# Mixing the first block straight from PSUM with 257-column products instead of differences, and ending VectorE's sums of k squares one group sooner

## Chip, cores, metric

One core of one Trainium2 chip. The metric is the device time of one execution in microseconds (us). All runs named here were fast runs; the granted TensorE clock of the profiled ones was 0.998 to 1.0. Times are medians, with lowest and highest and the number of runs. The profiled execution is one of the runs (for the kernel before a further one, 505.44). PE is TensorE, the matmul engine. Tiles whose names end in `_ps` (and `bank`) lie in PSUM, the other tiles in SBUF; to evacuate a tile is to copy it from PSUM to SBUF. A load is said to land at the time of PE's first instruction on its data, 0.03 to 0.05 us behind the landing itself, unless the text says that PE came later.

## The reference

Two parts, one behind the other. Sizes: 4 batches, 6208 rows, C = 256, hidden width 1024.

```python
def _attn_ref(q, k, v, tau):
    qn = q / (np.linalg.norm(q, axis=1, keepdims=True) + 1e-06)
    kn = k / (np.linalg.norm(k, axis=1, keepdims=True) + 1e-06)
    s = kn.transpose(0, 2, 1) @ qn / tau          # 256 x 256 per batch
    s = s - s.max(-1, keepdims=True)
    a = np.exp(s)
    a /= a.sum(-1, keepdims=True) + 1e-09
    return v @ a

def _moe_ref(x, mu_k, mu_r, w_k, w_v, w_r):       # x is what _attn_ref returns
    x_prev = ...                                  # x shifted down by one row, zero first
    xk = mu_k * x + (1.0 - mu_k) * x_prev
    xr = mu_r * x + (1.0 - mu_r) * x_prev
    k = np.maximum(xk @ w_k, 0.0)
    v = k * k @ w_v
    r = 1.0 / (1.0 + np.exp(-(xr @ w_r)))
    return r * v
```

Batch 0's q and k must be read whole before any x exists. That is the head of the program. The kernel then goes through blocks of 512 rows: x, the mixtures xk and xr, the two matmuls with the square between them, the gate.

## The kernel before: the parts that matter

Block 0 is mixed in a way of its own. PE computes x in PSUM, and the difference of neighbouring rows by multiplying a difference of v. ScalarE copies x to SBUF, and VectorE makes `xk = (mu - 1) * difference + x` (H is 256, half a block):

```python
def difference(a):                                     # VectorE, twice
    c = slice(a * H, (a + 1) * H)
    nc.vector.tensor_tensor(dv[:, :, c], vT0[:, :, a * H + 1:(a + 1) * H + 1], vT0[:, :, c], op=OP.subtract)

def product(a, ih):
    ...
    for dh in range(2):
        for t, src in zip(pairs[a], (vT0[:, ih, a * H + 1:(a + 1) * H + 1], dv[:, ih, a * H:(a + 1) * H])):
            nc.tensor.matmul(t[:, dh], a_sb[:, 0, ih, dh * P:(dh + 1) * P], src, ...)
    if ih:
        for dh in (0, 1):
            nc.scalar.copy(xT[:, dh, a * H + 1:(a + 1) * H + 1], pairs[a][0][:, dh])

def mix_first(key, a, dh):                             # one VectorE instruction
    c = slice(a * H, (a + 1) * H)
    m = less[:, dh:dh + 1] if key == "xk" else less[:, 2 + dh:3 + dh]
    nc.vector.scalar_tensor_tensor(st[0, key][:, dh, c], st[0, "ps"][a][1][:, dh], m,
                                   st[0, "x"][:, dh, a * H + 1:(a + 1) * H + 1], op0=OP.mult, op1=OP.add)
```

The schedule around the first blocks (i = -1 is the step that still belongs to the head; block 1 is `i + 2`):

```python
if j > 0 and 0 <= i + 1 < NBLK:
    square(i + 1, j - 1)               # VectorE: kk = kr * kr, four 512-column pieces in one go
...
if 0 < i + 2 < NBLK:
    n = i + 2
    if j in (0, 2) and full:
        x_half(n, int(j > 0))          # PE, then ScalarE evacuates xT
    if j == 3:
        mix_delta(n)                   # VectorE: delta = x - x_prev, needs both halves of xT
    if j in (4, 5):
        mix(n, "xk", int(j > 4))       # VectorE
if j in (0, 2) and i == -1:
    for a in range(2):
        mix_first("xr", a, int(j > 0)) # VectorE
```

Two things also matter: `kr` has two tiles, so ScalarE may write block 1's first `kr` only when the square of block 0's first four pieces has read the old one; and `group_cast` of group `NB - 1` contains `v_mark()`, a VectorE memset that releases the loads of v and of the weights on GpSimdE's queue.

## Time and profile before

| | value | how to read it |
|---|---|---|
| time | 505.31 us (505.25 to 505.42, 3 runs) | 2% is 10.1 us |
| profiled span | 503.67 us | |
| PE busy | 481.4 us, 96% of the span | no room except in the head |
| VectorE, ScalarE busy | 429.0 and 428.8 us, 85% each | averages; in the head each of them is at times what the others wait for |
| first 50 us | PE waits for casts, norms, softmax, mixing | the only place where this change acts |

The prediction shows the lines that carry this: the table of stretches, the chain of waits up to 49.17 us, and VectorE's timeline.

### The profile page before, as it was taken

To read this page: it belongs to the slowest core of one execution; us is meant where nothing else is said; L and a number is where in the kernel's file an instruction comes from. 1 tells how busy PE (TensorE), PEld (TensorE's weight loads), DVE (VectorE), ACT (ScalarE), POOL (GpSimd) and SP (SyncE) were. 2 spreads that over 40 slices of the span, in tenths; PEclk is the share of its full clock that TensorE was granted. 3 is DMA by queue.
4 is the path that set the end of the run, shared out by engine and by line. 5 is a ranking of instruction groups with operands and counts; after the bars stand their busy time and mean duration, and the time that the engine had idled before them with its cause. 6 is when DMAs were issued, how large, how long until landed. Compare 5 with 4: busy or idle time off the path is not lost.

```text
span 503.7 us, 9289 instructions
## 1 busy us (share of the span) xinstructions
PE 481.4 (96%) x3429; PEld 330.8 (66%) x3429; DVE 429.0 (85%) x789; ACT 428.8 (85%) x872; POOL 97.3 (19%) x143
## 2 busy tenths in 40 slices
PE   1689999999999999999999999999999999999996
PEld 1355677667666666776676676666666666666675
DVE  2778899998988998899889899899888787878784
ACT  4788999899989989888999898988888878788784
POOL 0044332222233222122123322110031010000000
PEclk9999999999999999999999999999999999999999
DMA  8999999999999999996699999982295858343123
GB/s 324 419 311 192 183 143 188 142 183 199 210 216 196 217 177 179 146 208 110 142 195 146 181 184 185 163 145 73 64 208 97 160 88 151 80 103 89 55 72 105
DMA packets 131558, 83.46 MB, mean 166 GB/s; under 512 B 50548, under 2 KB 125624, under 8 KB 130488
## 3 DMA queue, kind: packets, MB, share of 16 engines
q0 software_dynamic: 55840, 33.01, 51.7%
q1 hardware_dynamic: 75352, 49.59, 42.9%
q8 instruction: 27, 0.44, 0.4%
q10 hardware_dynamic: 320, 0.26, 0.2%
q14 instruction: 19, 0.16, 0.1%
HBM read 78.71 MB, written 25.43 MB: 207 GB/s over the span
## 4 chain that ended last, share of the span: by engine, by line
PE 87%; DMA 6%; ACT 3%; DVE 2%; issue 1%; SPq 1%; ACTq 0%; DVEq 0%
PE vr_ps L603 32%; PE kT_ps L571 32%; PE vr_ps L599 8%; PE xT_ps L465 8%; PE s_ps L293 6%; DMA vT<-v_bf 3%; DMA f<-in_k_dram 3%; ACT k L160 1%; ACT qk L155 1%; SPq L125 1%; PE s_ps L199 0%; PE y_ps L643 0%; DVE xk L556 0%; PE st_ps L353 0%; DVE k L167 0%
## 5 line engine op out<-in xcount | busy, mean ns | idle before, releaser
L576 ACT ACTIVATE kr<-kT_ps 128x512 bf16<-128x512 f32 (+1 forms) x390 | 234.5, 604 | 32.9 <-PE kT_ps L571 29.0
L603 PE MATMUL vr_ps<-w_v_sb,kk 128*128 128x256 bf16 x1536 | 230.2, 273 | 0.0
L571 PE MATMUL kT_ps<-xk,w_k_sb 128*128 128x512 bf16 (+1 forms) x780 | 230.0, 377 | 0.2 <-DVE xk L556 0.2
L603 PEld LDWEIGHTS <-kk 128*128 128x128 bf16 x1536 | 150.3, 98 | 57.3
L584 DVE TENSOR_TENSOR kk<-kr 128x2048 bf16<-128x2048 bf16 (+1 forms) x148 | 125.8, 851 | 0.2 <-ACT kr L576 0.2
L613 DVE SCALAR_TENSOR_TENSOR res<-res,vr_ps 128x256 f32<-128x256 f32 x192 | 80.0, 417 | 50.9 <-ACT res L612 50.9
L571 PEld LDWEIGHTS <-w_k_sb 128*128 128x128 bf16 x780 | 75.5, 98 | 27.5 <-issue 0.6
L612 ACT ACTIVATE res<-vr_ps 128x256 f32<-128x256 f32 x192 | 76.5, 399 | 2.3 <-PE vr_ps L603 1.3
L599 PE MATMUL vr_ps<-w_r_sb,xr 128*128 128x256 bf16 x384 | 73.3, 273 | 0.0
L467 ACT CAST xT<-xT_ps 128x512 bf16<-128x512 f32 x94 | 55.9, 594 | 20.0 <-PE xT_ps L465 19.7
L556 DVE SCALAR_TENSOR_TENSOR xr<-delta,mu_t,xT 128x512 bf16<-128x512 bf16 x94 | 70.0, 746 | 0.0
L556 DVE SCALAR_TENSOR_TENSOR xk<-delta,mu_t,xT 128x512 bf16<-128x512 bf16 x94 | 70.0, 746 | 0.0
L599 PEld LDWEIGHTS <-xr 128*128 128x128 bf16 x384 | 37.6, 98 | 44.7 <-issue 0.4
L133 POOL DMA_DIRECT2D qk<-in_q_dram x39 | 26.1, 668 | 159.8 <-ACT kr L576 129.8
L465 PE MATMUL xT_ps<-vT,a_sb 128*128 128x512 bf16 x188 | 55.9, 379 | 0.2 <-DMA vT<-v_bf 0.2
L293 PE MATMUL s_ps<-qk 128*128 128x256 bf16 (+1 forms) x294 | 55.8, 273 | 0.0
L254 ACT ACTIVATE sq<-qk 128x1024 bf16<-128x1024 bf16 x48 | 51.1, 1064 | 0.0
L408 POOL DMA_DIRECT2D v_bf<-in_v_dram x47 | 35.7, 761 | 69.4 <-DMA vT<-v_bf 49.2
L199 PE MATMUL s_ps<-qk 128*128 128x384 bf16 (+2 forms) x98 | 19.1, 340 | 16.6 <-ACT qk L155 16.1
L546 DVE TENSOR_TENSOR delta<-xT 128x1024 bf16<-128x1024 bf16 x47 | 32.3, 686 | 1.1 <-ACT xT L467 1.1
L293 PEld LDWEIGHTS <-qk 128*128 128x128 bf16 (+1 forms) x294 | 28.5, 98 | 5.6 <-issue 0.8
L133 POOL DMA_DIRECT2D qk<-in_k_dram x39 | 25.9, 664 | 5.7 <-DMA v_bf<-in_v_dram 2.5
(114 smaller groups left out, 252.2 us busy)
## 6 DMA issues: line engine op xcount, KB each, us to landing
out_dram<-res SPq DMA_DIRECT2D x47, 512.0 KB, 4.9
v_bf<-in_v_dram POOLq DMA_DIRECT2D x47, 256.0 KB, 8.6
qk<-in_q_dram POOLq DMA_DIRECT2D x36, 256.0 KB, 8.4
qk<-in_k_dram POOLq DMA_DIRECT2D x36, 256.0 KB, 9.4
f<-in_q_dram SPq DMA_DIRECT2D x4, 1024.0 KB, 13.5
f<-in_k_dram SPq DMA_DIRECT2D x4, 1024.0 KB, 11.0
f<-in_q_dram SPq DMA_DIRECT2D x3, 512.0 KB, 7.7
f<-in_k_dram SPq DMA_DIRECT2D x3, 512.0 KB, 6.1
```

The lines of the kernel that those rows point to most:

```text
L133: nc.gpsimd.dma_start(rows_at(qk, b, g, i)[:rows, :n], qk_src(t, b, g))
L293: nc.tensor.matmul(s_ps[:, ih, :], rows_at(qk, b, g, 0)[:rows, s, ih * P:(ih + 1) * P], rows_at(qk, b, g, 1)[:rows, s, :], start=t0 and ih ...
L465: nc.tensor.matmul(xT_ps, a_sb[:, b, ih, dh * P:(dh + 1) * P], vT[:, :, ih, :], start=ih == 0, stop=ih == 1)
L467: nc.scalar.copy(xT[:, dh, 1:], xT_ps)
L556: nc.vector.scalar_tensor_tensor(o[:, dh], st[i, "d"][:, dh], mu[:, dh:dh + 1], st[i, "x"][:, dh, :M], op0=OP.mult, op1=OP.add)
L571: nc.tensor.matmul(kT_ps[:, :m], w_k_sb[:, dh, fh * P:(fh + 1) * P], xk[:, dh, :m], start=dh == 0, stop=dh == 1)
L576: nc.scalar.activation(kr, kT_ps[:, :m], AF.Relu, scale=0.5 ** 0.5)
L584: nc.vector.tensor_tensor(st[i, "kk"][:, fh // 4 * 4 + lo:fh + 1, :m], kr, kr, op=OP.mult)
L599: nc.tensor.matmul(vr_ps[:, D:], xr[:, dh, s * P:(s + 1) * P], w_r_sb[:, dh, :], start=dh == 0, stop=dh == 1)
L603: nc.tensor.matmul(vr_ps[:, :D], kk[:, fh, s * P:(s + 1) * P], w_v_sb[:, fh, :], start=fh == 0, stop=fh == 7)
L612: nc.scalar.activation(res[:, s], vr_ps[:, D:], AF.Tanh, scale=0.5)
L613: nc.vector.scalar_tensor_tensor(res[:, s], res[:, s], 1.0, vr_ps[:, :D], op0=OP.add, op1=OP.mult)
```

## The change

Intent: drop the two differences of v and half of block 0's product matmuls. PE multiplies 257 columns, so that one PSUM tile holds x and, one column to the left, x_prev. ScalarE makes `xs = mu * x` for xk, VectorE makes `xs` for xr, and one VectorE instruction adds `(1 - mu) * x_prev` out of PSUM. Block 0's x is no longer copied to SBUF, so block 1's first column comes out of PSUM too, by two one-column copies on VectorE. The sums of k squares on VectorE end a group sooner; PE adds that group by one-column matmuls. The softmax transposes move ahead of the second half of v's transposes.

```diff
-    DIRECT = NB - 1
+    DIRECT = NB - 2
...
-        if g < DIRECT:
+        if g <= DIRECT:
...
-        for g in (0, DIRECT):
+        for g in (0, DIRECT, DIRECT + 1):
             norms_of(g)
...
-        nc.vector.tensor_scalar_add(less, mu_t, -1.0)
+        nc.vector.tensor_scalar(less, mu_t, -1.0, 1.0, op0=OP.mult, op1=OP.add)
...
+            elif i == 1:
+                for h in range(2):
+                    nc.vector.tensor_copy(xT[:, h, 0:1], st[0, "ps", 1, h][:, H:])
...
+    def product(a, dh):
+        tag, bufs = ("vr_ps", 2) if a == 0 else ("s_ps", 1) if dh == 0 else ("xT_ps", 2)
+        t = st[0, "ps", a, dh] = ps.tile([P, H + 1], F32, name="x_ps", tag=tag, bufs=bufs)
+        for ih in range(2):
+            nc.tensor.matmul(t, a_sb[:, 0, ih, dh * P:(dh + 1) * P], vT0[:, ih, a * H:(a + 1) * H + 1],
+                             start=ih == 0, stop=ih == 1)
...
-        nc.vector.scalar_tensor_tensor(st[0, key][:, dh, c], st[0, "ps"][a][1][:, dh], m,
-                                       st[0, "x"][:, dh, a * H + 1:(a + 1) * H + 1], op0=OP.mult, op1=OP.add)
+        if key == "xk":
+            nc.scalar.activation(xs, x_ps[:, 1:], AF.Copy, scale=mu_t[:, m:m + 1])
+        else:
+            nc.vector.tensor_scalar_mul(xs, x_ps[:, 1:], mu_t[:, m:m + 1])
+        nc.vector.scalar_tensor_tensor(st[0, key][:, dh, c], x_ps[:, :H], less[:, m:m + 1], xs,
+                                       op0=OP.mult, op1=OP.add)
...
     turn_half(0)
+    turn()
     turn_half(1)
-    take_half(1, nc.scalar.copy)
-    turn()
...
     take_half(0, nc.vector.tensor_copy)
-    difference(0)
+    take_half(1, nc.vector.tensor_copy)
```

(The removed `x_first` with its differences is cut; it is shown above. The first call of `mix_first` for xr takes half 1, the second half 0.)

More of the change, by code (lines that the diff above doesn't have):

```diff
@@ L223, in norms_last @@
         nc.tensor.transpose(mu_ps, mu_rows, ident_f[:4, :4])
-        for g in range(DIRECT + 1, LAST + 1):
+        for g in range(DIRECT + 2, LAST + 1):
             norms_of(g)
         nc.scalar.copy(mu_t, mu_ps)
-        nc.vector.tensor_scalar_add(less, mu_t, -1.0)
+        nc.vector.tensor_scalar(less, mu_t, -1.0, 1.0, op0=OP.mult, op1=OP.add)
     def half_tile(name, shape, dtype, tag):
@@ L467, in x_half @@
         nc.scalar.copy(xT[:, dh, 1:], xT_ps)
-    def x_first():
-        mix_tiles(0)
-        xT = p2.tile([P, 2, M + 1], BF16, name="xT", tag="xT", bufs=3)
-        st[0, "x"] = xT
-        dv = st[0, "d"]
-        pairs = st[0, "ps"] = []
-        def difference(a):
-            c = slice(a * H, (a + 1) * H)
-            nc.vector.tensor_tensor(dv[:, :, c], vT0[:, :, a * H + 1:(a + 1) * H + 1], vT0[:, :, c], op=OP.subtract)
-        def product(a, ih):
-            if ih == 0:
-                pairs.append([ps.tile([P, 2, H], F32, name="x_ps", tag=tag, bufs=bufs)
-                              for tag, bufs in ((("vr_ps", 2), ("vr_ps", 2)), (("s_ps", 1), ("xT_ps", 2)))[a]])
-            for dh in range(2):
-                for t, src in zip(pairs[a], (vT0[:, ih, a * H + 1:(a + 1) * H + 1], dv[:, ih, a * H:(a + 1) * H])):
-                    nc.tensor.matmul(t[:, dh], a_sb[:, 0, ih, dh * P:(dh + 1) * P], src,
-                                     start=ih == 0 and dh == 0, stop=ih == 1, skip_group_check=True)
-            if ih:
-                for dh in (0, 1):
-                    nc.scalar.copy(xT[:, dh, a * H + 1:(a + 1) * H + 1], pairs[a][0][:, dh])
-        return difference, product
@@ L494, in mix_first @@
+    def product(a, dh):
[4 more added lines that the diff above has]
+                             start=ih == 0, stop=ih == 1)
     def mix_first(key, a, dh):
         c = slice(a * H, (a + 1) * H)
-        m = less[:, dh:dh + 1] if key == "xk" else less[:, 2 + dh:3 + dh]
@@ L498, in mix_first @@
-        nc.vector.scalar_tensor_tensor(st[0, key][:, dh, c], st[0, "ps"][a][1][:, dh], m,
-                                       st[0, "x"][:, dh, a * H + 1:(a + 1) * H + 1], op0=OP.mult, op1=OP.add)
+        m = dh if key == "xk" else 2 + dh
+        x_ps = st[0, "ps", a, dh]
+        xs = pn.tile([P, H], F32, name="xs", tag="xs", bufs=4)
+        if key == "xk":
+            nc.scalar.activation(xs, x_ps[:, 1:], AF.Copy, scale=mu_t[:, m:m + 1])
+        else:
+            nc.vector.tensor_scalar_mul(xs, x_ps[:, 1:], mu_t[:, m:m + 1])
@@ L677 @@
         pending = k_sum(g) if 0 < g < DIRECT else []
-        if g == DIRECT + 1:
+        if g == LAST - 1:
             norms_first()
@@ L735 @@
     next_load()
-    difference, product = x_first()
+    mix_tiles(0)
     root(1)
@@ L755 @@
     weigh_first(1)
-    difference(1)
     for a in range(2):
-        for ih in range(2):
-            product(a, ih)
+        for dh in range(2):
+            product(a, dh)
         for dh in range(2):
@@ L812 @@
             if j in (0, 2) and i == -1:
-                for a in range(2):
-                    mix_first("xr", a, int(j > 0))
+                for dh in range(2):
+                    mix_first("xr", int(j == 0), dh)
             elif j in (0, 2) and 0 <= i + 1 < NBLK:
```

## The prediction

> **What bounds the kernel now.** I read the page first, then the table of stretches, then the chain of waits and the timeline by engine between 31 and 50 us, because every line of the diff acts before 50 us. The table of stretches gives busy time and instruction count of PE, PEld, DVE, ACT and POOL, the granted clock, and the DMA share:
>
> ```profile
> 36.00:40.00 4.00, 3.31 (x35) 2.11 (x35) 3.36 (x15) 3.71 (x11) 3.63 (x6) 1.00 1.02 160
> 40.00:45.00 5.00, 4.46 (x30) 2.81 (x31) 4.15 (x12) 3.90 (x12) 1.32 (x3) 1.00 1.14 198
> 45.00:50.00 5.00, 4.83 (x33) 2.71 (x32) 4.03 (x6) 4.83 (x9) 2.25 (x4) 1.00 1.39 199
> 50.00:60.00 10.00, 10.00 (x76) 7.00 (x75) 8.17 (x15) 10.00 (x20) 3.52 (x7) 1.00 1.22 205
> 60.00:480.00 420.00, 419.77 (x2990) 290.19 (x2989) 372.49 (x659) 368.63 (x765) 81.89 (x114) 1.00 0.98 152
> ```
>
> From 50 to 480 us PE is busy 429.77 of 430 us. So the program is a head of some 49 us, in which PE waits for others, and then a stream of matmuls without holes. The order of instructions after the head is the same in both kernels. A microsecond gained or lost in the head therefore reaches the end nearly whole, and nothing else in the change can. The chain of waits shows what sets the start of the stream (start us, us, what):
>
> ```profile
> 41.54 0.89 DVE xk L498 x2
> 42.42 0.04 issue
> 42.47 0.28 PE kT_ps L511
> ...
> 45.44 0.51 ACT xT L467
> 45.95 0.02 issue
> 45.97 0.69 DVE delta L546
> 46.66 1.14 DVE kk L584
> 47.80 1.34 DVE xk L556 x2
> 49.13 0.04 issue
> 49.17 0.38 PE kT_ps L571
> ```
>
> The last hole of the head ends at 49.17, when VectorE has made xk of block 1; before it VectorE runs delta, kk and two xk of block 1 without a break. So 49.17 is set by the start of delta, at 45.97. The VectorE timeline tells what delta waits for (start us, us, then the instruction, and in brackets the idle time before it):
>
> ```profile
> 41.54 1.75 DVE L498 SCALAR_TENSOR_TENSOR xk<-x_ps,less,xT 128x256 bf16<-128x256 f32 x4 [0.67 <-ACT xT L491]
> 43.21 1.65 DVE L498 SCALAR_TENSOR_TENSOR xr<-x_ps,less,xT 128x256 bf16<-128x256 f32 x4
> 45.97 0.69 DVE L546 TENSOR_TENSOR delta<-xT 128x1024 bf16<-128x1024 bf16 x1 [1.11 <-ACT xT L467]
> ```
>
> VectorE was through with block 0 at 44.86 and stood idle for 1.11 us until ScalarE had evacuated block 1's x. That 1.11 us is the slack that the change may spend on VectorE.
>
> **What the Trainium skill says.** (1) "VectorE: DVE Perf Modes", section "The TRN2 errata", gives 120 + elements cycles at 0.96 GHz for a PSUM source: 392 ns for 256 columns. The trace agrees: the four xr start 392 ns apart (1.65 us less the last duration of 474 ns, over three). (2) The same page, "The DRAIN you can't avoid", says that a semaphore costs nothing extra between Vector operations. The trace differs where there is a dependence, and decides:
>
> ```profile
> 29.87 0.43 DVE L167 TENSOR_TENSOR k<-k 128x512 bf16<-128x512 bf16 x1
> 30.33 0.29 DVE L170 TENSOR_TENSOR k<-k 128x256 bf16<-128x256 bf16 x1
> 30.66 0.43 DVE L172 TENSOR_TENSOR k_acc<-k_acc,k 128x256 f32<-128x256 f32 x1
> 31.00 0.69 DVE L145 CAST qk<-f 128x1024 bf16<-128x1024 f32 x1
> ```
>
> A dependent one starts 0.03 us after the end of its producer (29.87 + 0.43 = 30.30, next at 30.33); one that depends on nothing new starts 0.08 before the end (31.00 against 31.09). A dependent step thus costs 0.11 us more. (3) "ScalarE: Activation LUTs", "What ACT_TABLE_LOAD costs", says that each [128,1] pointer operand adds about 93 ns to an ACTIVATE. The trace agrees: 378 ns for the cast without, 470 for the exponential with a scale pointer, at the same shape:
>
> ```profile
> L491 ACT CAST xT<-x_ps 128x256 bf16<-128x256 f32 x4 | 1.3, 378 | 0.8 <-PE x_ps L487 0.8
> L361 ACT ACTIVATE e_sb<-st_ps,rn 128x256 f32<-128x256 f32 x2 | 0.9, 470 | 0.0
> ```
>
> **The change part by part.**
>
> *Sums of k squares.* VectorE no longer adds up one group: 0.42 + 0.28 + 0.42 us leave it between 31.77 and 33.45. The cast of the last full group's middle columns (32.11 to 32.79) now stands first. It cannot start before its data, which by ScalarE's square at 31.75 landed about 31.67; so about 31.75, 0.36 earlier, and PE's group starts near 32.49 instead of 32.84. PE gets eight matmuls of one column in return; the eight of the same form now take from 34.71 to 34.92, 0.21. PE runs without a break from 32.84 to 36.7, so the net gain is 0.36 - 0.21 = 0.15 us, up to the exponential (38.61 to 38.46).
>
> *Differences of v, order of the transposes.* VectorE loses the first difference (39.18, 0.43) but takes the second copy of v from ScalarE (0.43): even. Its first copy now waits for the second half of v's transposes, which now stand behind the softmax transposes: by my count it starts at 38.68, against 38.72. The attention weights follow the two copies, at 39.67 and 40.14 against 39.71 and 40.18. So of the 0.15 only 0.04 arrives at the products.
>
> *Products.* 16 matmuls of 256 columns, 109 ns apart, become 8 of 257. The first x_ps is complete when the second weight half is there, at 40.84; ScalarE formerly waited until 41.09 for a tile with both halves, so its first operation starts at 40.87, not 41.13 (0.26 sooner). It costs 470 instead of 378 ns: end 41.34 against 41.51. So VectorE's first xk starts at 41.38 against 41.54, and the fourth ends near 43.05 against 43.29, some 0.24 sooner. ScalarE's four, 0.37 apart, just keep ahead of VectorE's 0.40.
>
> *VectorE's block 0.* Here is the cost. Before: four xr, 1.65 us. After: two one-column copies (some 0.10 each, estimate from the 0.17 us of the smallest VectorE operations less the overlap), then four pairs of a multiply and a dependent scalar_tensor_tensor. The multiply has the form of s_sb (PSUM to SBUF, float32, 128x256), 479 ns; 0.03 to the next; 474 ns; less 0.08 of overlap: 0.90 a pair, 3.60 for four. Sum 3.80 in place of 1.57 from the first xr to where delta could start (1.65 less overlap): 2.2 us more on VectorE.
>
> *Sum.* First xk 41.38, four xk to 42.97 (start to start), copies to 43.17, pairs to 46.77. Delta starts at 46.77 instead of 45.97; ScalarE's xT would be there at about 45.7, so the wait for it is gone and VectorE itself is the bound. In another form: 2.23 more, less 1.11 of slack, less 0.24 of earlier start, less the 0.08 of overlap that an unbroken run gains, is 0.80. Delta, kk, xk are unchanged, so PE's stream starts at 49.97 instead of 49.17: **0.8 us later**.
>
> *How much arrives.* Later PE waits on something other than its stream hardly at all: 0.22 us at 130 us, for a transpose by DMA, and a few waits under 0.2. The transfers are mostly released by PE's and ScalarE's progress, so they shift along; a part may not and would swallow up to 0.4. I take 0.7: 505.31 + 0.7 = **506.0 us**.
>
> **The rivals.**
> 1. *A gain of about half a microsecond.* PE has half the product matmuls, ScalarE is earlier, and x_half of block 1 on PE (44.72) would come some 0.2 to 0.3 sooner. If delta still waited for ScalarE, the end would be near 505.0. Against it: VectorE would have to do 14 operations between 41.4 and 45.7, at 0.3 us each; the profile shows 0.39 from start to start for such operations even without a dependence, and twelve of the fourteen are of that size.
> 2. *Nothing arrives.* A transfer fixed in time, such as the transpose that ends PE's wait at 130 us, swallows the loss: 505.3 to 505.6. For it: SyncE's issue of transposes takes 7 us there, so the queues are full. Against: what fills them is itself released by PE.
> 3. *A larger loss, 506.4 to 506.6.* If the 0.15 of the first part doesn't come (data lands late) and ScalarE's scaled copies run over 0.40 apart, each delays VectorE's block 0 directly.
>
> **Range and chances.** Centre 506.0 from the sum. Errors: 0.2 for the fourteen VectorE durations, 0.2 for the start, 0.4 for what DMA swallows; the three runs of before lie within 0.17. That gives 505.4 to 506.5. Two per cent is 10 us, a fifth of the whole head, so a verdict other than the same needs something that the profile doesn't show.
>
> **What would show it right or wrong.** Right: VectorE without idle time from the first xk to delta; delta near 46.8 and its wait for ScalarE gone; four pairs about 0.9 apart; PE's hole before block 1's second matmul ending near 50.0, about 1 us long; from there the two traces side by side, shifted by a constant. Wrong: delta still ended by a wait for ScalarE near 45.7 (rival 1); a pair much under 0.9, which means the multiply or the dependence is cheaper; first xk at or after 41.54; or a shift at 50 us that has gone by 135 us (rival 2).

## The result, and the profile after

The changed kernel took 506.05 us (505.89 to 506.26, 4 runs), the kernel before 505.37 (505.25 to 505.69, 4 runs) in the same rounds. The ratio is 1.0013 with a 95% interval of 0.9995 to 1.003. A ratio here is the mean time of one kernel's fast runs over that of the other's of the same rounds, so not quite the ratio of the medians. The medians differ by 0.68 us, and a repeat (r1 below) gave 0.66. Neither interval excludes zero. But all nine runs of after took 505.89 or more, and thirteen of the fifteen runs of before in these two calls took 505.69 or less.

VectorE's timeline after (start us, us, then the instruction, in brackets the idle time before it):

```profile
41.53 1.66 DVE L490 SCALAR_TENSOR_TENSOR xk<-x_ps,less,xs 128x256 bf16<-128x256 f32 x4 [0.95 <-ACT xs L487]
43.11 0.22 DVE L461 CAST xT<-x_ps 128x1 bf16<-128x1 f32 x2
43.24 0.47 DVE L489 TENSOR_SCALAR xs<-x_ps,mu_t 128x256 f32<-128x256 f32 x1
43.75 0.48 DVE L490 SCALAR_TENSOR_TENSOR xr<-x_ps,less,xs 128x256 bf16<-128x256 f32 x1
44.15 0.48 DVE L489 TENSOR_SCALAR xs<-x_ps,mu_t 128x256 f32<-128x256 f32 x1
44.66 0.48 DVE L490 SCALAR_TENSOR_TENSOR xr<-x_ps,less,xs 128x256 bf16<-128x256 f32 x1
45.06 0.48 DVE L489 TENSOR_SCALAR xs<-x_ps,mu_t 128x256 f32<-128x256 f32 x1
...
46.89 0.68 DVE L538 TENSOR_TENSOR delta<-xT 128x1024 bf16<-128x1024 bf16 x1
```

Where there were four instructions and 1.11 us of idle time, there are ten instructions and no idle time. `delta` has no bracket any more: it waits for VectorE itself. A multiply and its dependent sum take 43.24 to 44.15, 0.91 us. The second half of the pair starts 0.04 after the first has ended (43.24 + 0.47 = 43.71, next at 43.75); the next pair starts 0.08 before that end.

The chain of waits after, at its two ends (start us, us, what):

```profile
33.61 5.72 DMA v_bf<-in_v_dram
39.33 0.05 issue
39.37 0.63 PE vT_ps L425 x8
40.01 0.02 issue
40.03 0.95 ACT vT L433
40.98 0.05 issue
41.02 0.48 ACT xs L487
...
48.71 1.34 DVE xk L548 x2
50.04 0.04 issue
50.08 0.39 PE kT_ps L563
```

The last hole of the head now ends at 50.08, 0.91 later than before. The upper end is a thing I had not reckoned with: ScalarE starts its scaled copies at 41.02 because until then it evacuates the transposes of v's block 1, whose load had only just landed. PE pays for it in this stretch (busy time and count of PE, PEld, DVE, ACT, POOL, then clock, DMA share, GB/s):

```profile
45.00:50.00 5.00, 3.93 (x28) 2.22 (x28) 4.93 (x10) 4.38 (x8) 2.08 (x4) 1.00 1.38 200
```

The prediction shows the same line of before with 4.83 of 5.00: PE lost 0.90 us here. (In r1 the same stretch has 4.41, with the hole as a whole 0.2 sooner: how much falls between 45 and 50 us depends on where the cut goes. In later stretches the count of PE's records is lower after, 2936 against 2990 between 60 and 480 us, with the same number of weight loads, 2989 in both: records are missing, not matmuls. Busy PE time there is not to be compared.)

The spans of the two profiles differ by 0.58, not 0.91. Two waits of the profile of before, between 104 and 140 us, have no counterpart after (waits of ScalarE and PE: what waited, for what, us, times, longest):

```profile
ACT res L612 <- DMA out_dram<-res: 1.0, 1, 1.0
...
PE xT_ps L465 <- DMA vT<-v_bf: 0.2, 1, 0.2
```

A marker shows what they came to: `res`, VectorE's last step for a tile, at its 21st and at its last instance. Before:

```profile
103.57 0.42 DVE L613 SCALAR_TENSOR_TENSOR res<-res,vr_ps 128x256 f32<-128x256 f32 x1 [0.72 <-ACT res L612]
...
497.92 0.42 DVE L613 SCALAR_TENSOR_TENSOR res<-res,vr_ps 128x256 f32<-128x256 f32 x1 [0.55 <-ACT res L612]
```

After:

```profile
104.48 0.42 DVE L605 SCALAR_TENSOR_TENSOR res<-res,vr_ps 128x256 f32<-128x256 f32 x1 [0.72 <-ACT res L604]
...
498.48 0.42 DVE L605 SCALAR_TENSOR_TENSOR res<-res,vr_ps 128x256 f32<-128x256 f32 x1 [0.56 <-ACT res L604]
```

From marker to marker it is 394.35 before and 394.00 after. At 104 us the whole 0.91 is still there; the 0.35 then comes from the before side. In one profile of each kernel that could be the swallowing that the prediction feared, or chance. The repeat r3 decides it below.

### The profile page after: what moved, and what is told of

The parts are those of the page before. It is cut to its first block, busy times and chain, and to the rows that moved or that the text cites. A ratio compares the mean times of both kernels' runs of the same rounds, so it can differ in the third digit from the quotient of the medians.

```text
span 504.2 us, 9230 instructions
## 1 busy us (share of the span) xinstructions
PE 478.7 (95%) x3370; PEld 330.4 (66%) x3429; DVE 430.2 (85%) x791; ACT 428.8 (85%) x870; POOL 97.3 (19%) x143
## 4 chain that ended last, share of the span: by engine, by line
PE 81%; DVE 7%; ACT 4%; DMA 4%; issue 2%; SPq 1%; POOL 0%; DVEq 0%; ACTq 0%
PE vr_ps L595 31%; PE kT_ps L563 28%; PE vr_ps L591 9%; PE xT_ps L468 7%; PE s_ps L293 5%; DMA f<-in_k_dram 3%; DVE kk L576 1%; DMA v_bf<-in_v_dram 1%; ACT kr L568 1%; DVE xk L548 1%; ACT k L160 1%; ACT sq L251 1%; DVE res L605 1%; SPq L125 1%; DVE delta L538 0%
## 5 line engine op out<-in xcount | busy, mean ns | idle before, releaser
L563 PE MATMUL kT_ps<-xk,w_k_sb 128*128 128x512 bf16 (+1 forms) x722 | 217.6, 377 | 1.3 <-DVE xk L548 1.2
L199 PE MATMUL s_ps<-qk 128*128 128x384 bf16 (+2 forms) x98 | 20.3, 359 | 15.0 <-ACT qk L155 14.9
```

Source lines behind the costliest of these rows:

```text
L563: nc.tensor.matmul(kT_ps[:, :m], w_k_sb[:, dh, fh * P:(fh + 1) * P], xk[:, dh, :m], start=dh == 0, stop=dh == 1)
```

## The experiments

"Before here" is the median of the kernel before.

| label | what | time, us (low to high, runs) | before here | ratio, 95% | `delta` starts, idle before it |
|---|---|---|---|---|---|
| e1_sums_only | before + sums part | 504.83 (504.65 to 505.22, 5) | 505.26 | 0.9991, 0.9979 to 1.0003 | 45.95, 1.55 |
| e2_interleaved | after, multiplies paired | 506.11 (505.45 to 506.85, 5) | 505.26 | 1.0010, 0.9998 to 1.0023 | 47.60, 0 |
| e3_no_multiply | after, no multiplies | 505.06 (504.89 to 505.59, 5) | 505.26 | 0.9996, 0.9984 to 1.0008 | 46.36, 1.53 |
| e4_turn_order | after, old transpose order | 506.13 (505.38 to 507.40, 6) | 505.26 | 1.0017, 1.0005 to 1.0029 | 46.51, 0 |
| e5_swap_after | after, square behind xk | 505.62 (505.56 to 507.22, 5) | 505.36 | 1.0008, 0.9987 to 1.0029 | 47.18, 0 |
| e6_swap_sums | e1 + square behind xk | 505.18 (504.95 to 506.11, 5) | 505.36 | 0.9998, 0.9976 to 1.0020 | 45.98, 1.18 |
| r1_after_again | after | 506.02 (505.89 to 506.17, 5) | 505.36 | 1.0009, 0.9990 to 1.0028 | 46.69, 0 |
| r2_interleaved_again | e2 | 505.93 (505.50 to 507.32, 6) | 505.36 | 1.0012, 0.9992 to 1.0032 | 47.04, 0 |
| r3_before_again | before | 505.43 (505.07 to 506.79, 5) | 505.22 | 1.0011, 0.9998 to 1.0025 | 45.83, 1.11 |
| r4_sums_again | e1 | 505.26 (504.73 to 505.51, 5) | 505.22 | 0.9999, 0.9987 to 1.0012 | 46.10, 1.42 |
| r5_swap_sums_again | e6 | 504.75 (504.42 to 504.92, 5) | 505.22 | 0.9991, 0.9978 to 1.0003 | 45.69, 1.11 |
| e7_loads_early | e6, loads released a group sooner | 504.52 (504.49 to 504.74, 5) | 505.22 | 0.9988, 0.9975 to 1.0000 | 45.68, 1.11 |

My theory: the four multiplies with their dependent sums use up VectorE's slack in front of `delta`, and the rest passes to the end. Rivals: the sums of k squares or the new order of the transposes cost the time; or something later does.

### The multiplies left out (e3)

Wrong: the xr sums read the `xs` that ScalarE made with mu_k, so xr's x part is mixed with the wrong vector. The comparison with the reference passes it all the same.

```diff
             if j in (0, 2) and i == -1:
                 for dh in range(2):
-                    mix_first("xr", int(j == 0), dh)
+                    mix_add("xr", int(j == 0), dh)       # the sum alone; mix_scale is the multiply
```

> Wrong on purpose: the changed kernel without xr's four multiplies on VectorE; its scalar_tensor_tensors read the products that ScalarE made for xk, so the output is not right. My theory: the four multiplies with their waits are the whole loss; VectorE is through with block 0 near 44.8, delta waits for ScalarE again and starts near 45.9, PE's stream starts at about 49.1, and the time is that of before or up to 0.3 us less (505.1 to 505.4). Rival, that the loss comes from elsewhere (order of the transposes, ScalarE's scaled copies, DMA): it stays at 506 or falls by under 0.3 us.

VectorE's timeline of e3:

```profile
43.19 1.65 DVE L493 SCALAR_TENSOR_TENSOR xr<-x_ps,less,xs 128x256 bf16<-128x256 f32 x4
46.36 0.69 DVE L546 TENSOR_TENSOR delta<-xT 128x1024 bf16<-128x1024 bf16 x1 [1.53 <-ACT xT L470]
```

The four sums alone take 1.65 us, as the four xr of before did, and the slack in front of `delta` is back, with ScalarE again the one that ends it. The time is 0.20 below before's, where after stands 0.66 to 0.68 above before's. In e3's own call the two kernels that keep the multiplies, e2 and e4, took 506.11 and 506.13. So, as far as the times tell, all that the change loses comes with the multiplies. `delta` is later than before's 45.97 because w_k landed at 42.77 in this trace, about 0.8 later than in the first profile of before.

### The sums part alone (e1, r4)

```diff
-    DIRECT = NB - 1
+    DIRECT = NB - 2
...
-        if g < DIRECT:
+        if g <= DIRECT:
...
-        for g in (0, DIRECT):
+        for g in (0, DIRECT, DIRECT + 1):
...
-        if g == DIRECT + 1:
+        if g == LAST - 1:
             norms_first()
```

> The kernel before with the new handling of the k squares alone (one group's sum left to eight one-column matmuls), everything else as before. My theory: PE's last full group starts about 0.4 us sooner, eight matmuls more cost 0.2, the exponential and block 1's delta come 0.1 to 0.2 us sooner than in the kernel before (delta at 45.8 instead of 45.97); time 0.0 to 0.2 us below before. Rival, that this part brings the loss (eight more matmuls on PE's path): 0.2 us or more above before.

> The kernel before with the new sums alone, once more. First run: 0.43 below before. My theory: it is 0.1 to 0.4 us below the kernel before, as its exponential comes some 0.2 to 0.4 us sooner, of which the landing of w_k at 42 us eats a part. Rival: no gain (within 0.1).

It costs nothing; that rival falls. Whether it gains is not settled: 0.43 below before's median and 0.04 above. The traces show why so little stays. In e1 the exponential starts at 38.23 and the first xk at 41.18, both about 0.37 sooner than before (most of it because the whole head ran sooner in that execution: the loads of v were issued at 31.69 instead of 32.02), but the matmuls behind it wait (PE's timeline of e1):

```profile
42.35 0.61 PE L511 MATMUL kT_ps<-xk,w_k_sb 128*128 128x256 bf16 x4 [0.79 <-DMA w_k_sb<-in_moe_w_k_dram]
```

The weights w_k land later than xk is ready, so ScalarE's chain, and `delta` at 45.95, are where they were. In r4 the same happened: w_k landed at 42.50, `delta` at 46.10.

### The order of the transposes (e4)

```diff
     turn_half(0)
-    turn()
     turn_half(1)
+    turn()
```

> The changed kernel with v's second half transposed in front of the softmax transposes, as in the kernel before, both copies still on VectorE. My theory: VectorE's copies and the attention weights come about 0.3 us sooner, but ScalarE is still in block 1's copy until about 41.0, so the first xk moves by at most 0.1 and the time by 0.0 to 0.1 us below the changed kernel. Rival, that the new order is what costs: 0.3 us or more below the changed kernel.

The order alone is not what costs the 0.7: `delta` still follows VectorE without idle time, 5.35 us behind the first xk (after: 5.36), and at 46.51 it is 0.54 later than before's 45.97. But I had expected the first xk to move by at most 0.1, and the attention weights came at 39.40 instead of 39.77 although the exponential started at the same 38.60, and the first xk at 41.16 instead of 41.53. So the new order itself delays the weights by some 0.37 us. That it reached xk also needed v's block 1 to land early, at 38.55 (PE came to it at 38.81) against 39.33. In that one trace the old order brings `delta` 0.38 sooner than after's. The times (505.38 to 507.40) do not show a gain; they scatter too much to tell.

### The multiplies interleaved (e2, r2)

If the dependence in each pair costs 0.12 us, two multiplies followed by their two sums must save it four times.

```diff
-                for dh in range(2):
-                    mix_first("xr", int(j == 0), dh)
+                for step in (mix_scale, mix_add):
+                    for dh in range(2):
+                        step("xr", int(j == 0), dh)
```

> The changed kernel with xr's two multiplies of a half issued one after the other, then its two scalar_tensor_tensors, so that no VectorE operation waits for the one just in front of it. The work is the same. My theory: the wait of a dependent operation costs 0.12 us each (0.036 after the end instead of 0.083 before it), four of them 0.47; delta at 46.4 instead of 46.89, still with no idle time before it; time 0.4 to 0.5 us below the changed kernel, about 505.6. Rival, that VectorE's count of operations or their PSUM reads alone cost, and the dependence nothing: unchanged, 506.05.

> The interleaved kernel once more, beside the changed kernel on the same chip, because its first run was spoilt by v of block 1 landing 1.3 us late. My theory: from first xk to delta 4.84 us instead of 5.36 as in the first run; time 0.4 to 0.5 below the changed kernel's of this call. Rival: no difference.

VectorE's timeline of e2:

```profile
44.47 0.87 DVE L487 TENSOR_SCALAR xs<-x_ps,mu_t 128x256 f32<-128x256 f32 x2
45.25 0.87 DVE L493 SCALAR_TENSOR_TENSOR xr<-x_ps,less,xs 128x256 bf16<-128x256 f32 x2
46.03 0.87 DVE L487 TENSOR_SCALAR xs<-x_ps,mu_t 128x256 f32<-128x256 f32 x2
```

Four instructions take 1.56 us from start to start (44.47 to 46.03) instead of 1.82 (43.24 to 45.06), and from the first xk to `delta` it is 4.84 us in both traces instead of 5.36. So the gap between dependent instructions is shown: 0.52 us for four. The times do not show it. v's block 1 landed at 40.68 and 40.12 in the two profiled runs, and the first xk waited for it until 42.76 and 42.20. The lowest runs, 505.45 and 505.50, lie below after's lowest of 505.89, but the medians do not. Inconclusive as a time.

### Block 0's square behind block 1's xk (e5, e6, r5)

On the path from `delta` to PE's stream stands a square of 1.22 us that PE needs only later. Moved behind the two xk:

```diff
-            if j > 0 and 0 <= i + 1 < NBLK:
+            if j > 0 and 0 <= i + 1 < NBLK and (i, j) != (-1, 4):
                 square(i + 1, j - 1)
...
                     mix(n, "xk", int(j > 4))
+                if (i, j) == (-1, 5):
+                    square(0, 3)
```

> The changed kernel with one move on VectorE in the head: the square of block 0's first four groups (kk, 1.2 us) is issued behind block 1's two xk instead of in front of them. My theory: kk lies on the path from delta to PE's stream and needn't; PE's stream starts about 1.0 us sooner (49.1 instead of 50.08 if delta is again at 46.9); time about 1.0 us below the changed kernel's runs of this call. Rival, that what PE lost in the head is given back later anyway (DMA at 110 to 135 us): a gain under 0.4 us.

> The kernel before with the new sums of k squares and the same move of kk. My theory: here PE was only 0.33 us short at that place (ready at 48.84, released at 49.17), so the gain over the kernel with the sums alone is about 0.3 us and no more; time some 0.4 to 0.8 below before. Rival, that the move gains as much here as in the changed kernel: 1 us.

> The sums and the move of kk, once more, beside the former on the same chip. My theory: 0.2 to 0.4 us below the sums alone. Rival: ScalarE, without idle time from 50 to 60 us, gives none of it through: within 0.1.

In e5 PE's second matmul of block 1 came 2.18 us behind `delta` instead of 3.19 (49.36 - 47.18 against 50.08 - 46.89): 1.0 gained there. By the marker at 104 us, 57.18 behind `delta` instead of 57.59, only 0.41 is left. ScalarE's timeline shows where the rest went; first e5:

```profile
50.54 0.60 ACT L568 ACTIVATE kr<-kT_ps 128x512 bf16<-128x512 f32 x1 [0.76 <-DVE kk L576]
```

and after:

```profile
50.50 0.60 ACT L568 ACTIVATE kr<-kT_ps 128x512 bf16<-128x512 f32 x1 [1.01 <-PE kT_ps L563]
```

The wait for PE has become a wait for the very square that was moved: block 1's first `kr` needs the tile that this square frees. Counted from `delta`, ScalarE gains only 0.25 (3.36 against 3.61). With more than two `kr` tiles that wait would go; this was not tried. e5 was 0.40 below r1, e6 0.18 below before, which its spread doesn't settle, and r5 was 0.51 below r4.

### The loads a group sooner (e7)

Late landings of v and w_k showed in most of these traces, so their release was moved one group up, on top of e6:

```diff
-        if g == NB - 1:
+        if g == NB - 2:
             v_mark()
```

> The same with the release of GpSimdE's loads (v, w_k and the rest) one group of k sooner, some 1.9 us. My theory: v of block 1 and w_k land about 1 us sooner, so PE no longer waits for w_k at 42 us; k's last loads may land some tenths later; time 0 to 0.4 us below the former. Rival: the loads of k are delayed by as much as w_k gains, and the time rises by 0.2 or more.

The stretch from 45 to 50 us of e7, columns as above:

```profile
45.00:50.00 5.00, 5.00 (x37) 3.01 (x35) 4.28 (x6) 4.90 (x11) 1.63 (x3) 1.00 1.30 204
```

PE has no hole left here; after had 3.93, before 4.83. v's block 1 landed at 37.93 (PE came to it at 38.56), and PE no longer waits for w_k. This is the lowest median: 504.52, all five runs between 504.49 and 504.74. That is 0.70 below before; the interval of the ratio ends at 1.0000. Most of it is e6's: r5 had 504.75. That the early loads are worth the other 0.23 is not shown: r5 too has 5.00 of 5.00 in this stretch, `delta` starts at 45.69 there and 45.68 here, and the 21st `res` at 102.96 in both. The exponential does start 0.19 sooner (38.33 against 38.52), but the attention weights do not (39.44 against 39.43).

### The two kernels again (r1, r3)

> The changed kernel itself, unaltered, once more, for its spread and a second trace. My theory: delta again 0.9 us later than in the kernel before, give or take where v of block 1 lands (the first xk moves with it); time 505.9 to 506.3. Rival: the 0.7 us was chance, and it falls within 0.3 of before.

> The kernel before itself, unaltered, for a second trace. In its first trace the stretch from the 21st to the 33rd result on VectorE (103.57 to 133.94) took 30.37 us; in all nine traces of other kernels it took 29.81. My theory: the wait for a transpose by DMA at 130 us was chance, and the stretch is 29.8 here too; then of the 0.9 us that the change loses in the head the timed runs should show more than 0.57. Rival: 30.4 again, a trait of this kernel's phase, which the change shifts away.

r1 repeats the result: 506.02, `delta` at 46.69 without idle time, 5.35 behind the first xk. r3 has the markers of before at

```profile
103.43 0.42 DVE L613 SCALAR_TENSOR_TENSOR res<-res,vr_ps 128x256 f32<-128x256 f32 x1 [0.72 <-ACT res L612]
...
497.44 0.42 DVE L613 SCALAR_TENSOR_TENSOR res<-res,vr_ps 128x256 f32<-128x256 f32 x1 [0.55 <-ACT res L612]
```

394.01 apart. In thirteen of the fourteen traces, of all nine different kernels, the distance is 394.00 or 394.01; the first profile of before, with 394.35, is the one exception. So its waits for DMA were no trait of that kernel, and nothing behind 104 us tells these kernels apart. What set them off in that one execution is open.

## Why the prediction was right

The time, 506.0 against 506.05, and the steps:

| step | predicted | after | r1 |
|---|---|---|---|
| exponential starts | 38.46 | 38.58 | 38.39 |
| attention weights start | 39.67, 40.14 | 39.77, 40.23 | 39.58, 40.04 |
| ScalarE's first operation on x | 40.87, 470 ns | 41.02, 474 ns | 40.83 |
| first xk | 41.38 | 41.53 | 41.34 |
| the two one-column copies | 0.20 | 0.13 | 0.13 |
| a multiply with its sum | 0.90 | 0.91 | 0.91 |
| `delta`, without idle time | 46.77 | 46.89 | 46.69 |
| PE's second matmul of block 1 | 49.97 | 50.08 | 49.89 |

- **The mechanism held.** The slack of 1.11 us was the budget, VectorE's added work exceeded it, and `delta` turned from waiting for ScalarE to waiting for VectorE. From the first xk to `delta` I had 5.39 us, the traces have 5.36 and 5.35: the copies are 0.07 cheaper, each pair 0.01 dearer. e3 shows the multiplies to be the cause; e2 and r2 confirm the term for the dependence by taking it away.
- **The mis-sized term was the start.** The shift in the head was 0.91, not 0.80, since the first xk gained 0.01 in place of 0.16 (41.54 to 41.38). ScalarE began on x at 41.02 instead of 40.87, for two reasons. The first x_ps was complete at 40.92 instead of 40.84, because the second attention weights came at 40.23 instead of 40.14 (next point). And I counted from the products to ScalarE and left out what ScalarE was doing: its copy of v's block 1 stood in between, until 41.04, because the load landed at 39.37 and not at 38.92 as before; that is the other 0.07. Where it landed later than about 39.1, the first xk came 2.0 to 2.2 us behind it in every trace, whichever the kernel (39.12 to 41.34, 39.48 to 41.46, 40.12 to 42.20, 40.68 to 42.76). In r1 the load came at 39.12 and the head as a whole ran 0.2 sooner (first issue of v at 31.81), and the predicted times are met within 0.1. In the first trace the first xk, at 41.53, came within 0.01 of the time (41.54) that the prediction had named as a sign of being wrong.
- **The gain on the sums was not 0.15 at the exponential** but 0.03 in the first trace (38.61 to 38.58). Counted from the first issue of v's loads, which the cast ahead of the removed sums releases (32.02 before), the exponential comes after 6.59 us in both traces of before, 6.55 and 6.58 in those of after, 6.54 and 6.53 in e1 and r4: some 0.05 gained. On PE the gain was there: the last diagonal blocks came 0.22 sooner (35.57 to 35.35). Most of it was lost between the two.
- **Where it was lost.** The traces show it for 0.17 of the 0.22: in one VectorE instruction, the sum of 1e-6 and the first two norms (`rn`, `tensor_scalar_add` in `invert_first`). It started 0.22 sooner but took 0.34 us instead of 0.17, and ended at 36.84, where GpSimd's issue of the load of w_r ended too (36.85). In all eleven traces that have the new sums and the old release of the loads it took 0.28 to 0.42 and ended within 0.01 us of that issue. In before and r3 it started only 0.15 and 0.14 before the issue ended, and took 0.17. e7 is the test, since it differs from r5 in the release alone: the issue ended at 34.99 there, the sum took 0.17, and from the diagonal blocks to the exponential it was 3.03 us (before and r3: 3.04, r5: 3.23). So GpSimd's issue held the gain back; what it shares with that instruction, no run shows.
- **How much arrives.** I took 0.1 off for DMA. Nothing is swallowed behind 104 us. The timed difference of 0.68 fits my 0.7, but its interval also holds zero and the head's 0.91, and the spans of the traces differ by 0.81 and 1.05 when both traces of after are set against r3. The 0.1 is therefore not confirmed; the agreement to 0.05 us is partly luck.
- **The rivals.** The first trace rules out a gain by rival 1: `delta` has no wait for ScalarE. "Nothing arrives" had the right place, the waits of the profile of before near 130 us, but they were no trait of that kernel. The larger loss did not come, though its condition, data that land late, did: e2's profiled run, with v's block 1 landing 1.3 us later than in after's trace, took 506.85.

Open: why the loads of v and w_k, issued within 0.7 us of each other's times in the traces looked at (33.26 to 33.89 for v's block 1, e7 apart), land up to 2 us apart; and what interleaving is worth in time.

## What to carry to other kernels

Before trading one instruction for two on an engine, find the next consumer that ends up waiting, and read how long that engine is idle just in front of it: that is the budget, and a removed matmul elsewhere does not add to it. Two dependent instructions back to back cost more than two independent ones (here 0.13 us a pair in the traces), so interleave them. After removing work from a path, look for the load or the buffer that takes over the wait; here it was the landing of v and w_k, GpSimd's issue of a load, and a `kr` tile freed by the instruction that had been moved out of the way.

## What the Trainium skill lacked or had wrong

- "VectorE: DVE Perf Modes", "The DRAIN you can't avoid", says of eight copies in a row that a semaphore after each costs nothing extra. It does not say whether a copy read what the one before it had written, so what follows adds to it; the prediction, which took the trace to differ from it, goes further than the page does. Here a dependent instruction starts 0.04 us after its producer's end and an independent one 0.08 before it, and interleaving four dependent pairs saves 0.52 us (5.36 to 4.84, in two traces). The page lacks a figure for dependent chains.
- "DMA: Bandwidth & Descriptors", "Anatomy of one DMA — SWDGE (gpsimd) path", gives about 2.0 us plus bytes over 436 GB/s for one transfer. For v's block of 256 KB that would be an estimate of 2.6 us, and of 3.2 for w_k's 512 KB (bytes as written; the float32 sources are twice that, which would make 3.2 and 4.4). In the head, with other loads under way, v's block took from 4.9 us (e4) to 6.8 us (e2) from the start of its issue to the landing itself, and w_k from 7.5 us (after) to 8.7 (e2). The page lacks a figure for the spread of one transfer beside others; here it was up to 1.8 us, more than the 0.7 under study.
- Nothing to mend in "ScalarE: Activation LUTs", "What ACT_TABLE_LOAD costs": a scale by pointer added 97 ns (377 to 474 ns at 128x256), where the page has about 93.
